# Four steps of a two-stage kernel issued later: a value tile's scaling, its loads, a weight conversion, a group's norms

## The chip, the cores and the metric

One NeuronCore of a Trainium2 chip runs the whole program. The metric is the device time in microseconds (us) of one execution; before the change the median of three runs is 522.26 us (521.84 to 522.62). The engines are called as in the profile: PE is TensorE's matrix multiply and PEld its weight load, DVE is VectorE, ACT is ScalarE, POOL is GpSimd, and SP is the engine that here only issues DMAs. Every engine works through its own instructions in program order; semaphores order them against one another.

## What is computed

A delta rule over 4 batches and 8 heads, with sequences of 768 steps and heads of 48 elements, followed by a feed-forward layer with a maximum of three products:

```python
k_n = k / (norm(k) + 1e-6)
for t in range(S):
    y[t] = q[t] @ state
    state += beta[t] * outer(k_n[t], v[t] - k_n[t] @ state)
x = y.transpose(0, 2, 1, 3).reshape(B * S, H * D)      # 3072 x 384
h = maximum(maximum(x @ w1, x @ w2), x @ w3)           # 3072 x 768
out = h @ w_out                                        # 3072 x 384
```

## The kernel before

**Stages.** The sequence is cut into 12 chunks of 64 steps; two chunks form a group, of which there are six. For a chunk the recurrence becomes products of 64x64 matrices: Gram matrices of keys and queries (`gram`), the inverse of a triangular matrix (`solve`, for a whole group at once, 31 elimination steps of two DVE instructions each, L552 and L556), and then a chain of small matmuls by name: `halves_z`, `halves_u`, `join_z`, `join_u` finish the inverse; `old_k` (p_k, L731) and the subtraction of L743 form the right-hand side in the value tile; `new` (p_u, L759) makes u, copied out by ACT at L764; `step` (p_s, L782) adds to the state at L789; `to_y` (p_y) and `to_x` (p_x) give the layer's input xt. The values have to be multiplied by the norms of their keys first: `scale` (L287) on POOL, called directly or by `prep_values`.

**The layer.** `ffn(m)` is a generator for group m. Each `yield` ends a piece: three matmuls p_h (L914, recorded as six) and what takes them out of PSUM, an ACT copy for the first of a triple (L922), a DVE maximum for the others (L928). For the first group there are 18 pieces 256 wide (pieces 0 to 17, over the blocks f = 0, 1, 2 twice), nine 512 wide (18 to 26), then four output pieces. PSUM has two buffers for p_h and three for the pairs of banks that the chunk's products share.

**Weights.** They come as 64-bit floats and are converted in the kernel, in 24 parts (`pieces`). `fetch` loads one part (L215) into one of five `w_bits` buffers, on the queue given. Each `some(conv, 1)` makes ACT read the next part (L238 to L240) into one of two `mant` buffers, and then issues the previous part's `joined`: a shift on DVE (L250) and an addition on POOL (L254). So the weights of part p are ready only after the call for part p + 1. Piece i of the first nine uses part i.

**The order is written out by hand.** Up to L1065 stands a straight list for group 0. Then the loop of L1126 runs over the pieces of `ffn(0)`, and after each piece issues what tables give for its number: `FIRST` for the second chunk (`queries`; `S1` is one elimination step of `solve(1)`), `EARLY_LINKS` for the group after it, `CONVERTED` for conversions, `FETCHED` for loads on POOL, and single conditions for loads of keys, queries and values. As all engines keep program order, a line's place in the loop is its place in each queue that it uses. A wait of one instruction holds everything issued after it on that engine.

**The places in question.** `load_v` has three value buffers and two DMAs per call (L139), on SP where nothing else is said. `load_v(1)` is issued on POOL at L1038, `scale(1)` follows at L1052. `solve` begins with `norm`: a square root on ACT (L261) of a tile that comes by DMA (`blocks`, L483), then a chain of short DVE instructions. `solve(2)` is begun in piece 20, ahead of "j1 u0", that is of `join_u(3)` (copied out at L716) and `new(2)`.

Of the kernel before, what the change touches and what calls it, by code (L numbers as in the profile page):

```python
# [23 lines left out]
def kernel(  # L24
# [31 lines left out]
    nc = tc.nc  # L56
# [52 lines left out]
    def rows(bb):  # L109
        return slice(C * bb, C * (bb + 1))  # L110
# [6 lines left out]
    def load(src, dst, n, queues):  # L117
        c, g = divmod(n, 2)
        for bb in range(2):
            queues[bb].dma_start(  # L120
                out=dst[rows(bb ^ g), :, 0:D],
                in_=src[2 * bb + g, :, c * C : (c + 1) * C, :].rearrange(
                    "h p d -> p h d"
                ),
            )

    def place(n):
        return n % NK if n < 12 else n % 4

    def load_k(n, queues=one_queue):  # L130
        load(k, kpad[place(n)], n, queues)

    def load_q(n, queues=one_queue):
        load(q, qpad[n % NQ], n, queues)

    def load_v(c, queue=nc.sync):
        vts[c] = work.tile([128, 2, H, D], FP32, name="v_t", bufs=3)
        for bb in range(2):
            queue.dma_start(  # L139
                out=vts[c][rows(bb)].rearrange("p g h d -> p (g h) d"),  # L140
                in_=v[2 * bb : 2 * bb + 2, :, c * C : (c + 1) * C, :].rearrange(
                    "b h p d -> p (b h) d"
                ),
            )
# [66 lines left out]
    def fetch(queue=nc.scalar):  # L211
        if fetched[0] < len(pieces):
            _, src, (a, b) = pieces[fetched[0]]
            st = work.tile([128, 2 * 384], U32, name="w_bits", bufs=5)
            queue.dma_start(  # L215
                out=st.rearrange("p (a b) -> p a b", a=a), in_=src
            )
            staged.append(st)
            fetched[0] += 1

    def weights():

        waiting = None
        for dst, _, (a, b) in pieces:
            bits = staged.popleft().rearrange("p (a b two) -> p a b two", a=a, two=2)
            low, high = bits[:, :, :, 0], bits[:, :, :, 1]
            mant = work.tile([128, 384], U32, name="mant", bufs=2)
            up = work.tile([128, 384], I32, name="up", bufs=2)  # L230
            mant_v = mant.rearrange("p (a b) -> p a b", a=a)
            up_v = up.rearrange("p (a b) -> p a b", a=a)
            halves = [
                up.bitcast(t)[:, i::2].rearrange("p (a b) -> p a b", a=a)
                for i, t in enumerate((I16, FP16))
            ]

            nc.scalar.mul(mant_v.bitcast(FP32), high.bitcast(FP32), 2.0**-112)  # L238
            nc.scalar.mul(halves[0], low, 2.0**-29)
            nc.scalar.mul(halves[1], high.bitcast(FP32), 2.0**-64)  # L240
            if waiting:
                joined(*waiting)
            waiting = dst, mant, mant_v, up_v
            yield
        joined(*waiting)
        yield
# [39 lines left out]
    def scale(c, nrm):  # L286
        nc.gpsimd.tensor_tensor(  # L287
            out=vts[c], in0=vts[c],
            in1=nrm[:, :, :, None].to_broadcast([128, 2, H, D]), op=ALU.mult,
        )  # L290

    def prep_values(c):

        if c in nrms:
            scale(c, nrms.pop(c))


    nrm_0 = const.tile([128, 2, 2, H], FP32, name="nrm_0")
# [8 lines left out]
    def square(name):  # L307
        return work.tile([128, H, C], FP32, name=name, tag="square", bufs=17)
# [180 lines left out]
    def placed(cc, i, copy=nc.vector.tensor_copy, xs_of=slice(0, 2 * H)):  # L489
        bb, half = divmod(i, 2)  # L490
        r = block(bb, half)
        to = ut[cc][r, :, :, BL * half : BL * (half + 1)].rearrange(
            "p g h i -> p (g h) i"
        )
        of = in_rows(xs[0])[r, :, 16 * cc : 16 * (cc + 1)].rearrange("p i x -> p x i")
        copy(to[:, xs_of], of[:, xs_of])
# [130 lines left out]
    def halves_t(c, parts=(0, 1)):  # L627
        if c not in fine:
            fine[c] = [square("t") for g in range(2)]
        src = [ut[c % NU][:, g].rearrange("p h x -> p (h x)") for g in range(2)]  # L630
        dst = [t.rearrange("p h x -> p (h x)") for t in fine[c]]
        if 0 in parts:
            nc.vector.transpose(out=dst[0], in_=src[0])
        for bb in range(2) if 1 in parts else ():
            nc.vector.transpose(out=dst[1][rows(1 - bb)], in_=src[1][rows(bb)])
# [42 lines left out]
    def halves_u(c):  # L678
        t, z = fine.pop(c), zs[c % NU]
        for hs, p_v, negate in negated_of(c, "p_f", BL):  # L680
            for i, h in enumerate(hs):
                for bb, g in TILES:
                    r = rows(bb ^ g)
                    nc.tensor.matmul(p_v[bb][rows(bb), g, i], t[g][r, h], z[r, g, h])
            for f in (0, 1):
                for bb in range(2):
                    r = block(bb, f, HB)
                    negate[bb](
                        ut[c % NU][r, :, span(hs), BL * f + HB : BL * (f + 1)],
                        p_v[bb][r, :, :, HB * f : HB * (f + 1)],  # L690
                        -1.0,
                    )
# [267 lines left out]
    def some(gen, n):  # L960
        for _ in range(n):
            if next(gen, gen) is gen:
                break

    conv = weights()
    solving = solve(0)
# [68 lines left out]
    blocks(1, nc.gpsimd)  # L1035
    for _ in range(2):
        fetch(nc.gpsimd)
    load_v(1, nc.gpsimd)  # L1038
    halves_u(0)
    turn_t1(0)  # L1040
    join_z(0)
# [7 lines left out]
    new(0)  # L1049
    some(conv, 1)  # L1050
    fetch(nc.gpsimd)
    scale(1, nrm_0[:, 1])  # L1052
    placed(1, 3)
    halves_t(1, (0,))
    to_y(0)
    halves_t(1, (1,))
    solving = solve(1)
    some(solving, 1)
    to_x(0)
    fetch(nc.gpsimd)  # L1060
    some(conv, 1)
    fetch(nc.sync)
    some(conv, 1)
    load_q(4)
    load_v(2)  # L1065

# [31 lines left out]
    def links(m, names):  # L1100
        for name in names.split():
            f, i = name[0], int(name[1])
            if f in RECURS and m < GROUPS:
                RECURS[f](2 * m + i)
            elif f in MADE and m + 1 < GROUPS:
                MADE[f](2 * (m + 1) + i)
            elif f in UNIT and m + 1 < GROUPS:
                UNIT[f](4 * (m + 1) + i)
            elif f == "N" and m + 2 < GROUPS:
                load_blocks(4 * (m + 2) + i)  # L1110
# [10 lines left out]

    CONVERTED = {0, *range(2, 6), *range(11, 25)}
    FETCHED = {8: 1, 12: 1, 13: 1, 14: 1, 18: 2, 19: 2, 20: 1, 21: 1}
    for i, _ in enumerate(ffn(0)):  # L1126
        if 0 < i < 7:
            fetch(nc.sync)
        for _ in range(FETCHED.get(i, 0)):
            fetch(nc.gpsimd)  # L1130
        if i == 25:
            some(conv, 1)
        if i == 20:
            solving = solve(2)
            some(solving, 1)
        if i == 21:
            some(solving, 3)
        queries(FIRST.get(i, ""))
        links(1, EARLY_LINKS.get(i, ""))
        if i in CONVERTED:  # L1140
            some(conv, 1)
        if 3 < i < 14:
            some(solving, (3, 2, 2, 2, 3, 3, 3, 3, 2, 2)[i - 4])
        if i in (5, 7):
            prep_values(i // 2)
        if i in (1, 7):
            for n in range(2):
                load_k(8 + 2 * (i > 1) + n, (nc.gpsimd, nc.gpsimd))
        if i == 0:
            load_v(3)  # L1150
        if i in (0, 2):
            load_q(5 + i // 2)
        if i == 11:
            load_q(11, (nc.gpsimd, nc.gpsimd))
        if i in (10, 21):
            load_v(4 + i // 21)
        if i == 18:
            blocks(2)
        if i == 23:
            prep_values(4)  # L1160
        if i > 21:
            some(solving, (3, 2, 3, 2, 2, 5, 5, 5, 4)[i - 22])
        if i in (27, 28, 29):
            load_blocks(i - 15, nc.sync)
        if i in (15, 17, 19, 22, 25, 27):
            less_first((15, 17, 19, 22, 25, 27).index(i))
        if 27 <= i < 30:
            turn_first((2 * (i - 27), 2 * (i - 27) + 1))
# [5 lines left out]
    for m in range(1, GROUPS):  # L1174
        for i, _ in enumerate(ffn(m)):
# [4 lines left out]
            if m + 2 < GROUPS:  # L1180
                if i == 6:
                    blocks(m + 2)
                if i == 8:
                    solving = solve(m + 2)
# [32 lines left out]
```

## Time and profile before

| what | value |
|---|---|
| median of three runs | 522.26 us |
| the profiled execution's own time | 526.19 us |
| its span, first to last instruction | 524.5 us |
| PE busy | 499.9 us, 95% |
| DVE busy | 304.3 us, 58% |
| POOL busy | 191.6 us, 37% |
| ACT busy | 162.8 us, 31% |
| mean granted TensorE clock | 0.954 |

The profiled execution is 3.93 us longer than the median; 1.7 us of its time lie around the span. Sections of the page give busy time by engine, the span in 40 slices (13.1 us each, a digit is tenths), the DMA queues, the chain that ended last, and groups of instructions by line. A timeline row reads: start, duration, engine, line, operation, tile written from tile read, how many; in brackets the idle time of the engine ahead of it and what ended it. A row of waits reads: who waited for whom, total us, times, longest. A row of windows gives the window, its length, the busy time of PE, PEld, DVE, ACT and POOL with their counts, the granted TensorE clock (1.00 is full), the busy share of the DMA engines, and GB/s.

### The profile page before, as it was taken

How to read it: one execution, taken by the hardware profiler on the slowest of the kernel's cores; microseconds unless marked ns; L12 is line 12 of the kernel's file. 1: busy time of each engine (PE TensorE's matmuls, PEld its weight loads, DVE VectorE, ACT ScalarE, POOL GpSimd, SP SyncE). 2: the span in 40 equal slices, each digit the busy share in tenths (PEclk: the TensorE clock that was granted, in tenths of full speed). 3: DMA queues.
4: the chain of work that ended last, by engine and by line, in shares of the span. 5: the costliest groups of instructions: out<-in, count | busy, mean ns of one | idle time of the engine just before them, and what ended most of it. 6: DMA issues, size and time to landing. Idle time of an engine off the chain costs nothing.

```text
span 524.5 us, 18004 instructions
## 1 busy us (share of the span) xinstructions
PE 499.9 (95%) x7836; PEld 309.5 (59%) x7836; DVE 304.3 (58%) x690; ACT 162.8 (31%) x302; POOL 191.6 (37%) x315
## 2 busy tenths in 40 slices
PE   7778699998999999999999999999999999999996
PEld 6666478855656555565555565555665555654453
DVE  5888659875996361599662998554897231111100
ACT  5574664884422142210152200252201411011000
POOL 7444424682374662872295780502230000000000
PEclk9666879997999999999999999999999999999999
DMA  8939939565026762554485453834333202220011
GB/s 110 210 74 188 208 97 165 160 146 167 15 51 163 163 123 52 127 134 114 106 164 119 116 136 92 165 53 91 85 101 94 43 2 63 57 65 0 0 28 32
DMA packets 105565, 53.45 MB, mean 102 GB/s; under 512 B 89712, under 2 KB 99344, under 8 KB 105488
## 3 DMA queue, kind: packets, MB, share of 16 engines
q1 hardware_dynamic: 94016, 31.94, 30.2%
q0 software_dynamic: 9360, 19.98, 16.0%
q8 instruction: 61, 1.00, 0.8%
q10 hardware_dynamic: 2112, 0.39, 0.5%
q14 instruction: 16, 0.13, 0.1%
HBM read 39.17 MB, written 13.11 MB: 100 GB/s over the span
## 4 chain that ended last, share of the span: by engine, by line
PE 86%; DMA 5%; SPq 2%; DVE 2%; ACT 2%; issue 1%; POOL 1%; POOLq 0%; ACTq 0%
PE p_h L914 39%; PE p_o L946 25%; PE p_g L406 4%; DMA v_t<-in_v_dram 3%; PE p_u L759 2%; PE p_m L894 2%; PE p_k L731 2%; PE p_q L731 2%; PE p_y L801 2%; PE p_s L782 2%; SPq L120 2%; PE p_j L714 2%; PE p_z L701 1%; DMA w_bits<-in_moe_w_dram 1%; PE p_t L329 1%
## 5 line engine op out<-in xcount | busy, mean ns | idle before, releaser
L914 PE MATMUL p_h<-xt,w_sb 128*128 128x512 f32 (+1 forms) x522 | 222.4, 571 | 0.7 <-ACT xt L827 0.6
L914 PEld LDWEIGHTS p_h<-xt,w_sb 128*128 128x128 f32 x522 | 97.6, 196 | 87.1 <-issue 79.6
L946 PE MATMUL p_o<-wo_sb,h 128*128 128x384 f32 x288 | 97.8, 489 | 0.0
L928 DVE TENSOR_TENSOR h<-h,p_h 128x512 f32<-128x512 f32 (+1 forms) x48 | 29.7, 618 | 95.9 <-PE p_h L914 93.9
L946 PEld LDWEIGHTS p_o<-wo_sb,h 128*128 128x128 f32 x288 | 53.7, 190 | 35.7 <-issue 0.5
L556 DVE TENSOR_TENSOR y_bl<-y_bl,tmp 128x31 f32<-128x31 f32 (+20 forms) x139 | 52.5, 378 | 4.8
L952 ACT COPY o_sb<-p_o 128x384 f32<-128x384 f32 x24 | 11.5, 479 | 134.2 <-PE p_o L946 128.1
L552 DVE TENSOR_TENSOR tmp<-x_bl,y_bl 128x31 f32<-128x31 f32 (+20 forms) x139 | 50.1, 360 | 4.1
L924 ACT ACTIVATE h<-p_h 128x512 f32<-128x512 f32 x30 | 17.9, 597 | 87.6 <-PE p_h L914 86.1
L946 PE MATMUL p_o<-w_sb,xt 128*128 128x384 f32 x120 | 42.0, 486 | 0.0
L364 POOL DMA_DIRECT2D turned<-in_q_dram x72 | 39.3, 554 | 4.7 <-POOL turned L359 3.1
L254 POOL TENSOR_TENSOR w_sb<-mant,up 128x384 int32<-128x384 int32 x18 | 19.0, 1060 | 39.5 <-DVE mant L250 37.9
L946 PEld LDWEIGHTS p_o<-w_sb,xt 128*128 128x128 f32 x120 | 22.8, 190 | 15.9
L406 PEld LDWEIGHTS p_g<-kqt 48*64 48x64 f32 x1216 | 24.4, 140 | 11.1 <-issue 6.3
L406 PE MATMUL p_g<-kqt 48*64 48x64 f32 (+1 forms) x1216 | 27.8, 240 | 2.2 <-ACT kqt L335 2.2
L120 POOL DMA_DIRECT2D kpad<-in_k_dram x32 | 21.9, 694 | 15.0 <-PE p_s L782 14.1
L789 DVE TENSOR_TENSOR st<-st,p_s 48x768 f32<-48x768 f32 (+1 forms) x18 | 17.1, 950 | 16.5 <-PE p_s L782 16.3
L139 POOL DMA_DIRECT2D v_t<-in_v_dram x14 | 11.6, 832 | 35.0 <-PE p_u L759 35.0
L390 DVE TENSOR_TENSOR pt<-p_g,mask 128x512 f32<-128x512 f32 x20 | 13.8, 691 | 17.4 <-PE p_g L406 17.4
L287 POOL TENSOR_TENSOR v_t<-v_t,nrm 128x768 f32<-128x768 f32 x12 | 17.9, 1498 | 14.8 <-DVE nrm L281 8.9
L359 POOL MEMSET turned<- 128x96 f32 x18 | 3.3, 192 | 48.9 <-DVE kqt L380 48.9
L743 DVE TENSOR_TENSOR v_t<-v_t,p_k 128x768 f32<-128x768 f32 x11 | 10.5, 951 | 15.0 <-PE p_k L731 15.0
(142 smaller groups left out, 616.9 us busy)
## 6 DMA issues: line engine op xcount, KB each, us to landing
out_dram<-o_sb SPq DMA_DIRECT2D x48, 96.0 KB, 2.2
w_bits<-in_moe_w_dram SPq DMA_DIRECT2D x10, 384.0 KB, 7.5
turned<-in_q_dram POOLq DMA_DIRECT2D x72, 48.0 KB, 2.8
w_bits<-in_moe_w_dram POOLq DMA_DIRECT2D x8, 384.0 KB, 5.8
kpad<-in_k_dram POOLq DMA_DIRECT2D x32, 96.0 KB, 4.9
y_x<-y SPq DMA_DIRECT2D x16, 192.0 KB
qall<-y_x SPq DMA_DIRECT2D x32, 96.0 KB, 3.0
v_t<-in_v_dram POOLq DMA_DIRECT2D x14, 192.0 KB, 5.4
```

The source lines that it names most:

```text
L120: queues[bb].dma_start(out=dst[rows(bb ^ g), :, 0:D], in_=src[2 * bb + g, :, c * C : (c + 1) * C, :].rearrange("h p d -> p h d"),)
L254: nc.gpsimd.tensor_tensor(out=dst.bitcast(I32), in0=mant_v.bitcast(I32), in1=up_v, op=ALU.add)
L287: nc.gpsimd.tensor_tensor(out=vts[c], in0=vts[c], in1=nrm[:, :, :, None].to_broadcast([128, 2, H, D]), op=ALU.mult,)
L364: (queue, nc.gpsimd)[i].dma_start(out=t[p0 : p0 + 32, bb, at : at + NP * 2 * D].rearrange("p (j x) -> p j x", j=NP), in_=(k, q)[i][2 * bb ...
L406: nc.tensor.matmul(p_g[rows(bb ^ (g * i)), par, c0 : c0 + C * (1 + whole)], kq[:, 0], kq if whole else kq[:, i],)
L552: nc.vector.tensor_tensor(out=t_v, in0=row.to_broadcast(t_v.shape), in1=column.to_broadcast(t_v.shape), op=ALU.mult,)
L556: nc.vector.tensor_tensor(out=rest, in0=rest, in1=t_v, op=ALU.subtract)
L731: nc.tensor.matmul(p_b[rows(bb), par, c0 : c0 + D], kqt[g][dims(par), j, bb ^ g, i], st[dims(par), bb ^ g, g, j],)
L914: nc.tensor.matmul(p_h, w_sb[i][:, t, f * 128 : (f + 1) * 128], xt[:, t, lo : lo + w], start=(t == 0), stop=(t == KT - 1),)
L924: nc.scalar.activation(out=h, in_=p_h, func=mybir.ActivationFunctionType.Relu)
L928: nc.vector.tensor_tensor(out=h, in0=h, in1=p_h, op=ALU.max)
L946: nc.tensor.matmul(p_o, stays, moves, start=(n == 0), stop=(n == len(terms) - 1))
```

## The change

In the straight list, `load_v(1)` moves from L1038 to the place of `scale(1)` (L1052), and `scale(1)` moves into piece 0 of the loop. The first output's copies (`to_y(0)`) come ahead of both halves of `halves_t(1)`. One `fetch` on POOL, one conversion call and `load_v(2)` leave the list; the fetch comes back on SP in piece 0, the conversion in piece 6, so that every conversion from the fifth to the tenth is issued one place later in the loop. `load_v(2)` comes in piece 3, `load_v(3)` in piece 9 instead of 0, their scalings in pieces 8 and 13 instead of 5 and 7. Keys 8 and 9 load in piece 4 instead of 1, keys 10 and 11 in piece 8 instead of 7. `solve(2)` begins behind `links` of piece 20 instead of ahead of it. No instruction is added or left out.

```diff
@@ straight list
     for _ in range(2):
         fetch(nc.gpsimd)
-    load_v(1, nc.gpsimd)
     halves_u(0)
...
     fetch(nc.gpsimd)
-    scale(1, nrm_0[:, 1])
+    load_v(1, nc.gpsimd)
     placed(1, 3)
-    halves_t(1, (0,))
     to_y(0)
-    halves_t(1, (1,))
+    halves_t(1)
     solving = solve(1)
     some(solving, 1)
     to_x(0)
-    fetch(nc.gpsimd)
     some(conv, 1)
     fetch(nc.sync)
-    some(conv, 1)
     load_q(4)
-    load_v(2)
@@ loop over ffn(0)
-    CONVERTED = {0, *range(2, 6), *range(11, 25)}
+    CONVERTED = {0, *range(2, 7), *range(11, 25)}
...
-        if 0 < i < 7:
+        if i < 7:
             fetch(nc.sync)
+        if i == 0:
+            scale(1, nrm_0[:, 1])
...
-        if i == 20:
-            solving = solve(2)
-            some(solving, 1)
         if i == 21:
             some(solving, 3)
         queries(FIRST.get(i, ""))
         links(1, EARLY_LINKS.get(i, ""))
+        if i == 20:
+            solving = solve(2)
+            some(solving, 1)
         if i in CONVERTED:
             some(conv, 1)
...
-        if i in (5, 7):
-            prep_values(i // 2)
-        if i in (1, 7):
+        if i in (8, 13):
+            prep_values(i // 4)
+        if i in (4, 8):
             for n in range(2):
-                load_k(8 + 2 * (i > 1) + n, (nc.gpsimd, nc.gpsimd))
-        if i == 0:
-            load_v(3)
+                load_k(8 + 2 * (i > 4) + n, (nc.gpsimd, nc.gpsimd))
...
-        if i in (10, 21):
-            load_v(4 + i // 21)
+        if i in (3, 9, 10, 21):
+            load_v((3, 9, 10, 21).index(i) + 2)
```

## The prediction

> **What bounds the kernel now.** I read the 40 slices first, for where TensorE is not full.
>
> ```profile
> PE   7778699998999999999999999999999999999996
> ...
> PEclk9666879997999999999999999999999999999999
> ```
>
> From slice 10 (131 us) on PE is full at full clock, and what is saved ahead of that is kept. The chain that ended last has its non-PE pieces between 30 and 55 us, at 63 to 67 and at 120 to 125. Second, the waits of 40 to 70 us:
>
> ```profile
> ACT mant L238 <- POOL w_sb L254: 6.0, 1, 6.0
> POOL v_t L287 <- DMA v_t<-in_v_dram: 5.8, 1, 5.8
> PE p_j L714 <- issue: 3.6, 1, 3.6
> PE p_f L684 <- ACT z L676: 2.5, 1, 2.5
> ```
>
> Third, the timeline of each pause, in order of time:
>
> ```profile
> 49.13 1.57 POOL L287 TENSOR_TENSOR v_t<-v_t,nrm 128x768 f32<-128x768 f32 x1 [5.84 <-DMA v_t<-in_v_dram]
> ...
> 52.51 0.54 ACT L238 ACTIVATE mant<-w_bits 128x384 f32<-128x384 f32 x1 [5.95 <-POOL w_sb L254]
> ...
> 54.80 1.14 PE L684 MATMUL p_f<-z,t 64*64 64x32 f32 x64 [2.50 <-ACT z L676]
> ...
> 66.42 0.31 PE L714 MATMUL p_j<-z,t 32*32 32x32 f32 x11 [3.56 <-issue]
> ```
> ```profile
> 122.92 0.26 ACT L261 ACTIVATE root_bl<-x_bl 128x32 f32<-128x32 f32 x1 [4.40 <-DMA x_bl<-at_d]
> ...
> 124.42 0.80 ACT L764 COPY u<-p_u 128x768 f32<-128x768 f32 x1
> ...
> 125.27 1.96 PE L782 MATMUL p_s<-u,kmore 64*64 64x48 f32 x64 [2.37 <-ACT u L764]
> ```
>
> Pause A: POOL sits before the second values' scaling until their load lands; the join of weight part 2 queues behind it, ACT's next conversion needs that join's buffer, and the copies of h and z queue behind the conversion, so p_f starts at 54.80. Pause B: 53 matmuls into p_j PE stops for 3.56 us with nothing that it waits for. Pause C: ACT sits before group 2's root; the copy of u, done waiting at 119.5, stands behind it.
>
> Last, windows cut at the clock's steps:
>
> ```profile
> 52.97:56.38 3.41, 1.58 (x108) 1.58 (x111) 1.00 (x2) 3.41 (x9) 2.71 (x4) 1.00 1.28 223
> 56.38:59.80 3.42, 3.42 (x42) 2.44 (x34) 2.42 (x7) 1.16 (x4) 1.45 (x3) 0.51 1.27 158
> 59.80:63.21 3.41, 3.05 (x124) 2.36 (x124) 3.12 (x9) 2.28 (x5) 0.00 (x0) 0.99 1.16 229
> 63.21:66.62 3.41, 0.20 (x11) 0.20 (x10) 3.27 (x9) 0.80 (x2) 0.99 (x1) 1.00 1.18 263
> 66.62:70.03 3.41, 3.41 (x78) 3.02 (x69) 0.89 (x3) 2.52 (x5) 1.00 (x1) 0.51 0.35 88
> ```
>
> A window with PE busy for 1.58 or 0.20 of 3.41 us is followed by half clock, for one window after pause A, for two after B and C; one with 3.05 is not. At half clock a 256-wide piece takes 2.86 us instead of 1.30 to 1.49, p_u 1.89 instead of 1.08. A pause costs its length and then this.
>
> **The straight list.** With to_y ahead of halves_t, DVE's copy of y no longer stands behind a transpose: it starts when p_y ends (41.84) instead of at 42.40, and piece 0 at 44.6 instead of 45.16. The transpose then comes later on DVE, ahead of a norm that starts at 44.4 either way: free. The value load is issued on POOL from 43.3 (end of the fetch at 42.54 + 0.76), two DMAs of 0.84, the last at 44.1. Its landing is the unknown. Bounds: 5.4 us (the page's median for this load on POOL) and 9.4 (this load in the trace). I take 7.9, nearer the crowded row, for the DMA engines' share is over 1.0 here, although SP's 11.02 us of issuing two value tiles are gone. It lands at 52, scaled at 53.6.
>
> POOL joins part 2 as soon as DVE has shifted it, behind the norm (48.8 + 0.35): 49.2 to 50.2, before 52.4. ACT copies h at 47.5, z at 49.9, then converts. p_f follows piece 1 at 51.7, before 54.80; p_k ends at 54.0. The subtraction of L743 needs p_k and the scaled values: 54.3, before 57.21. So 2.9 us are won here, not the 5.84 that POOL sat; each us that the load lands after 52.7 takes one back.
>
> **The conversion one place later** takes most of the rest's slack. Part 4's shift now stands at the end of piece 2's list on DVE. The same list took from 57.21 (L743) to 63.71 (shift): 6.5 us, then 0.35 for the shift, 1.0 on POOL. From 54.3: 62.3 with 0.1 between. PE meanwhile does piece 2, p_z and piece 3 until 57.7, waits for t's transposes (54.3 + 4.55 = 58.85), does p_j and p_q until 60.5, and sits until 62.3: piece 4 starts there, before 68.55. That is a new wait of 1.8 us in place of the old ones. Behind it part 5 is ready at 65.6 by the same count; PE then goes on without a wait through p_u, p_t, piece 5, p_y, piece 6, p_s, piece 7 and p_x, to piece 8 at 74.3, before 81.81: 7.5 us.
>
> Clock: 60.5 to 62.3 leaves a window as busy as 1.6 of 3.4 us, like the row with 1.58. The Trainium skill (TensorE: Matmul & The Clock Gate, Part 1: The HAM clock gate) lets the clock fall only after at least one idle window of about 3.4 us; by that rule a pause of 1.8 costs nothing and the 7.5 stand. The row shows the fall after 1.8 idle us, so I follow the row. Half clock from 63.2, for two windows as in two of the three cases: the end of piece 4, p_u 1.96, p_t 0.74, piece 5 2.9, p_y put piece 6 at 71.0 instead of 68.3: 2.7 lost. Left: 4.8.
>
> **Pause B.** The instruction queue of PE's size (61 packets of 16 KB for 15,672 instructions, 257 each, so one for 128 matmuls and their loads) had a packet at 55.4 and the next at 63.6, inside the pause; the next came at 67.5, just behind it. I read B as a late instruction packet among the loads. The skill says against it that crossing a block is mostly hidden (Runtime: NRT & Kernel Launch, Instruction fetch mechanics); then B has another cause and need not go. In 43 to 66 us the change removes two value tiles (0.79 MB) and four key DMAs (0.39 MB) of about 5 MB moved. I take B as gone; if it stays, 3.56 us from 59.3 lie mostly in the new wait and cost 2.0 beyond it. So the sum takes nothing for B by itself.
>
> **Loads moved.** Keys 8 to 11: four DMAs of 0.69 = 2.76 us of POOL each time, in its idle times of 2.5 to 8.0 us between joins (64 to 93); landing 4.9, needed at pieces 10 to 15. Their waits for the keys' last readers (p_s of pieces 0 and 6) are long over. Values 2 and 3 on SP: behind the fetches, which wait for ACT's conversions; tile 2 has five pieces, tile 3 four (83.55 to 93.82, 10.3 us) against 7.0 to 9.4 to land. Scalings of 1.5 in pieces 8 and 13, in POOL's 8.0 idle us. All at nothing; without that cover, up to 1.5 a scaling and 2.8 for keys, as joins behind them slip. The fetch on SP instead of POOL: 0.6, both idle; nothing.
>
> **Pause C.** The copies of p_j and u no longer stand behind the root: 1.19 + 0.80 from 118.4, u at 120.5, so p_s follows p_g at 122.9 instead of 125.27. The root still runs at 122.9 (its tile's DMA is not moved) and now holds the conversion and h of piece 21, ready at 125.3, needed for piece 23 at 127.4: hidden. What is late next is DVE: its list from 123.21 is unchanged and has no idle time but 0.67 and 0.2 until 167. Its sum to the state ends at 131.3, so p_k starts there instead of at 135.49; L743 ends at 138.2, so p_u starts there instead of at 141.21: 3.0. From piece 25 on 2.8 are left, as the last maximum (151.11, now some 0.7 earlier) comes just at p_o's last term. Bounds: 1.5 if half clock follows the pauses of 1.1 us at p_k and p_u, 4.6 if DVE does not hold.
>
> **Sum.** 4.8 + 2.8 = 7.6 off the profiled execution's 526.19 is 518.6. That execution is 3.9 above the median, and nothing shows where; if it lies in pause B, the timed runs have less to give (below). Off the median: 514.7.
>
> **Rivals.** (1) The clock doesn't fall in the new wait: 7.5 + 2.8 = 10.3, 512.0; for it stands that its windows may fall elsewhere. (2) Pause B is not there, or smaller, in the timed runs, or stays after: with it gone from the kernel before, p_q would end at 64.3 and piece 5 start at 67.4, some 1.5 us behind the new one: 1.5 + 2.8 = 4.3, 518.0; with it staying, 2.8 + 2.8, 516.7. For it: the 3.9 us, and that one packet in seventeen stalls. (3) DVE takes back C too and the load lands at its bound of 9.4 or later: within 1 us of before. (4) Slower: the value load, now issued 4.4 us later behind three weight parts, lands very late. Behind its scaling on POOL queue part 3's join and all later ones, on DVE L743 with all elimination steps and shifts after it. Each us past 52.7 costs one; the 7.6 are used up at a landing of 60.3, and at 62 the time is 524.0. Against it: no load of values in the trace took over 9.4, and this would be 18.
>
> **How the numbers follow.** Likeliest 0.42: 514.7. Rival 1 0.18: 512.0. Rival 2 0.25: 516.7 to 518. Rival 3 0.07, rival 4 0.08. A measurement of this kernel tells about 0.2% (1.0 us) from no change. Faster 0.87, the same 0.05, slower 0.08. The range goes from C's upper bound with rival 1 (510.5) to 520.5, beyond rival 2 with C at its lower bound; it leaves out the end of rival 3 and rival 4.
>
> **What would show it.** Right: POOL's scaling begins at 51 to 54; p_f at about 52 with no wait for z; no wait of ACT for the root ahead of u, p_s at once behind p_g; a PE wait of 1 to 3 us for weights (w_sb, L254) at piece 4. Wrong: the instruction pause of over 2 us still in 50 to 70; DVE's L743 waiting for v_t; pause C giving more than 4.6 or less than 1.5 us; PE pauses behind 131 us that before has not.

## The result, and the profile after

| | before | after |
|---|---|---|
| median, timed side by side | 522.05 us (521.65 to 522.62) | 518.03 us (517.15 to 518.73) |
| ratio, 95% interval | | 0.9921, 0.9903 to 0.9940 |
| the profiled execution's own time, span | 526.19, 524.5 us | 517.84, 515.9 us |

The change makes the kernel 4.1 us (3.1 to 5.1) faster; 7.6 were forecast, and the time lies in the range. Between the two profiled executions the difference is 8.35 us, twice as much. Which of the two is to be explained is the first thing that the runs had to settle. (The ratios below leave out the runs that took over 1.5% longer than the fastest of their kernel, at most two of twelve but four with values only, so they are not the quotients of the medians beside them.)

Two rows of the page after, the 40 slices, answer to the first that were shown of before:

```profile
PE   7877799999999999999999999999999999999996
...
PEclk9657889999999999999999999999999999999999
```

Counted from 0, PE is full from slice 5 (64 us) on and at full clock from slice 6 (77 us); the clock's dip of slice 9 (118 to 131 us) in the profile before is gone. The timeline of the pauses after:

```profile
40.81 1.41 PE L759 MATMUL p_u<-v_t,ut 64*64 64x48 f32 x42 [1.45 <-issue]
...
53.44 1.09 PE L684 MATMUL p_f<-z,t 64*64 64x32 f32 x59 [1.87 <-issue]
...
64.32 2.70 PE L914 MATMUL p_h<-xt,w_sb 128*128 128x256 f32 x6 [1.69 <-POOL w_sb L254]
```
```profile
54.48 1.47 POOL L287 TENSOR_TENSOR v_t<-v_t,nrm 128x768 f32<-128x768 f32 x1 [1.74 <-DMA v_t<-in_v_dram]
```
```profile
115.70 0.80 ACT L764 COPY u<-p_u 128x768 f32<-128x768 f32 x1
116.40 0.26 ACT L261 ACTIVATE root_bl<-x_bl 128x32 f32<-128x32 f32 x1
```

The pause inside p_j is gone. p_f no longer waits for the copy of z, but PE now stops 22 matmuls into chunk 0's p_u and 3 into p_f, again with nothing that it waits for. Piece 4 waits 1.69 us for its weights, as forecast (1.8). POOL's scaling begins at 54.48 instead of the forecast 52, and the root no longer waits at all. Windows of after, cut at the clock's steps:

```profile
61.17:64.58 3.41, 1.72 (x109) 1.56 (x96) 3.27 (x9) 3.35 (x7) 1.00 (x1) 1.00 0.23 60
64.58:67.99 3.41, 3.41 (x46) 2.42 (x49) 2.80 (x9) 1.29 (x3) 1.00 (x1) 0.50 1.12 210
67.99:71.40 3.41, 3.41 (x110) 2.91 (x104) 2.73 (x7) 2.77 (x6) 3.28 (x5) 1.00 0.53 132
```

The window with the new wait has PE busy for 1.72 us and is followed by one at half clock, not two.

A table of where PE stands (start of the first matmul, us) in profiles of before and after carries most of what follows. The last column is the length of the stretch from piece 8 to the first p_o, which holds pause C and nothing of pauses A and B:

| profile | piece 4 | piece 8 | p_s of chunk 2 | first p_o | piece 8 to p_o |
|---|---|---|---|---|---|
| before | 68.55 | 81.8 | 125.27 | 150.7 | 68.9 |
| after | 64.32 | 76.9 | 117.76 | 141.1 | 64.2 |

Read by these two profiles, 4.9 us come from before piece 8 (forecast 4.8) and 4.7 from pause C (forecast 2.8, upper bound 4.6). Of the latter 0.9 is lost again behind the first p_o: from there to the end of the span it is 373.8 us before and 374.8 after.

### The profile page after: what moved, and what is told of

It is laid out like the page before. It is cut to its first block, busy times and chain, and to the rows that moved or that the text cites. A ratio compares the mean times of both kernels' runs of the same rounds, so it can differ in the third digit from the quotient of the medians.

```text
span 515.9 us, 18005 instructions
## 1 busy us (share of the span) xinstructions
PE 494.3 (96%) x7836; PEld 306.2 (59%) x7836; DVE 303.4 (59%) x690; ACT 162.5 (32%) x302; POOL 190.2 (37%) x314
## 4 chain that ended last, share of the span: by engine, by line
PE 81%; DVE 7%; ACT 4%; DMA 2%; SPq 2%; issue 2%; POOL 1%; DVEq 0%; ACTq 0%; POOLq 0%
PE p_h L914 35%; PE p_o L946 26%; PE p_g L406 3%; PE p_u L759 3%; PE p_m L894 2%; PE p_k L731 2%; PE p_y L801 2%; PE p_s L782 2%; SPq L120 2%; PE p_q L731 1%; PE p_j L714 1%; DMA w_bits<-in_moe_w_dram 1%; PE p_z L701 1%; DMA kmore<-in_k_dram 1%; PE p_t L329 1%
## 5 line engine op out<-in xcount | busy, mean ns | idle before, releaser
L914 PE MATMUL p_h<-xt,w_sb 128*128 128x512 f32 (+1 forms) x522 | 218.0, 562 | 2.4 <-POOL w_sb L254 1.7
L914 PEld LDWEIGHTS p_h<-xt,w_sb 128*128 128x128 f32 x522 | 95.6, 192 | 87.1 <-issue 78.1
L552 DVE TENSOR_TENSOR tmp<-x_bl,y_bl 128x31 f32<-128x31 f32 (+20 forms) x139 | 51.5, 370 | 4.1
L556 DVE TENSOR_TENSOR y_bl<-y_bl,tmp 128x31 f32<-128x31 f32 (+20 forms) x139 | 48.5, 349 | 4.8
L759 PEld LDWEIGHTS p_u<-v_t,ut 64*64 64x64 f32 x768 | 13.8, 146 | 10.5 <-issue 8.7
```

What stands on the lines that cost most here:

```text
L552: nc.vector.tensor_tensor(out=t_v, in0=row.to_broadcast(t_v.shape), in1=column.to_broadcast(t_v.shape), op=ALU.mult,)
L556: nc.vector.tensor_tensor(out=rest, in0=rest, in1=t_v, op=ALU.subtract)
L759: nc.tensor.matmul(p_v[rows(bb ^ g), g, i], ut[c % NU][rows(bb), g, h], rhs[rows(bb), g, h],)
L914: nc.tensor.matmul(p_h, w_sb[i][:, t, f * 128 : (f + 1) * 128], xt[:, t, lo : lo + w], start=(t == 0), stop=(t == KT - 1),)
```

## The experiments

**The kernel before once more, and pause C alone.** The first theory was rival 2 with pause C: the long stop in p_j is chance, and the timed gain is mostly C's.

> The kernel before, unchanged, profiled a second time. First theory: the 3.56 us instruction pause inside p_j is chance, and the timed runs mostly go without it: this profile has less than 1.5 us there, piece 5 starts near 67.4 to 69 us instead of 73.87, and the execution's time is near 522. Rival: the pause belongs to this order of loads and is in every run: again 3 us or more inside p_j, piece 5 near 74, time near 526, and the 3.9 us between profile and median are the profiler's.

Unchanged, one profile: 522.92 us.

> The kernel before with solve(2) alone moved behind links of piece 20. First theory: the pause of 2.4 us at p_s and the half clock behind it go, 2.8 to 4.6 us faster than before (ratio 0.991 to 0.995), so most of the whole change's 4.0 us. Rival (the gain lies in the loads, and DVE takes this one back): less than 1.5 us.

```diff
-        if i == 20:
-            solving = solve(2)
-            some(solving, 1)
...
         links(1, EARLY_LINKS.get(i, ""))
+        if i == 20:
+            solving = solve(2)
+            some(solving, 1)
```

> The changed kernel with solve(2) put back ahead of links in piece 20. First theory: what the moves around 40 to 80 us give when the kernel before has no long instruction pause: 0 to 1.5 us faster than before (ratio 0.997 to 1.000); the wait of 2 to 2.5 us at p_s is there again. Rival: 3 us or more faster, as the profiles' 4.9 us at piece 8 say.

The same five lines, undone in the changed kernel.

| kernel | median | before beside it | ratio, 95% interval | profile: piece 8 | piece 8 to p_o |
|---|---|---|---|---|---|
| before again | 522.92 (one) | | | 82.4 | 64.6 |
| solve moved alone | 522.30 | 521.41 | 1.0014, 0.9984 to 1.0044 | 83.0 | 64.4 |
| solve put back | 517.34 | 521.41 | 0.9924, 0.9897 to 0.9952 | 74.7 | 64.1 |

The theory fell on both points. Moving solve(2) alone gains nothing (0.7 us slower, from 0.8 faster to 2.3 slower). With it put back, the rest of the change gives 4.0 us (2.5 to 5.4), the whole gain. And the stop for no visible reason is no single event. The timeline of PE in the second profile of before:

```profile
59.81 1.36 PE L914 MATMUL p_h<-xt,w_sb 128*128 128x256 f32 x3 [2.71 <-issue]
...
67.33 0.42 PE L714 MATMUL p_j<-z,t 32*32 32x32 f32 x11 [2.49 <-issue]
```

and in that of solve moved alone:

```profile
67.86 0.42 PE L714 MATMUL p_j<-z,t 32*32 32x32 f32 x11 [4.50 <-issue]
```

It comes always with 11 matmuls of p_j left, for 3.56, 2.49 and 4.50 us, and in the last two profiles PE stops a second time, 3 matmuls into piece 2 (2.71 and 0.25 us). From p_f's third matmul to piece 2's third are 61 + 64 + 3 = 128, from there to p_j's 53rd 3 + 64 + 6 + 53 = 126: one instruction packet's worth of 128 matmuls within two. That fits a late instruction packet at each place, and the traces hold the packets too. In the first profile of before, the packet that belongs to the stop in p_j landed at 64.83 us, and PE went on at 66.42; in the second, packets landed at 58.24 and 65.70, and PE went on at 59.81 and 67.33. In all fourteen profiles together PE stops 24 times for over 0.2 us at such places between 36 and 72 us, and each stop ends 1.3 to 1.9 us after its packet has landed. So PE stops for its instructions.

What became of pause C stands in ACT's rows. The root in the second profile of before, then in that of solve put back:

```profile
121.69 0.26 ACT L261 ACTIVATE root_bl<-x_bl 128x32 f32<-128x32 f32 x1 [1.93 <-DMA x_bl<-at_d]
121.97 1.18 ACT L716 ACTIVATE ut<-p_j 32x512 f32<-32x512 f32 x2
123.18 0.80 ACT L764 COPY u<-p_u 128x768 f32<-128x768 f32 x1
```
```profile
114.05 0.26 ACT L261 ACTIVATE root_bl<-x_bl 128x32 f32<-128x32 f32 x1 [1.73 <-DMA x_bl<-at_d]
...
115.54 0.80 ACT L764 COPY u<-p_u 128x768 f32<-128x768 f32 x1
```

The root's tile was issued at 114.51 in the first profile of before and used 8.4 us later; here the issues are at 116.00 and 108.12, 5.7 and 5.9 us earlier than the root. With 2.5 to 2.7 us less of DMA the copy of u still comes behind the root, but p_s waits for it not at all here and for 0.57 us with solve put back, and the clock stays full. So the pause that the first profile priced at over 4 us is hidden here behind piece 21 and p_g. One later profile (loads alone, below) has it again, with the tile 7.1 us under way: ACT waits 3.17 us, p_s 1.72, half clock follows, and the last column of the table is 67.2. With solve(2) moved PE has another wait: in all eight such profiles p_u of chunk 3, between 131 and 138 us, waits 0.66 to 1.00 us for L743, and in none of the other six.

**The conversions earlier.** What does the new wait at piece 4 cost?

> The changed kernel with the conversion calls of pieces 2 and 3 issued ahead of those pieces' other work, so that DVE's shifts of weight parts 4 and 5 no longer stand behind transposes, a mask and elimination steps. First theory (piece 4 waits for the late conversion, 1.69 us and half clock behind it): the wait at piece 4 falls below 0.5 us, the clock stays full there, and the time is 1.5 to 4 us below the changed kernel's (ratio to before 0.985 to 0.989). Rival (the slack is eaten by the instruction packets or by DVE): the wait turns up under another name, and the time is within 1 us of the changed kernel's.

```diff
+        if i in (2, 3):
+            some(conv, 1)
         queries(FIRST.get(i, ""))
...
-        if i in CONVERTED:
+        if i in CONVERTED - {2, 3}:
```

515.92 us, ratio 0.9915 (0.9883 to 0.9947). The wait of piece 4 is gone from the profile, piece 8 stands at 76.0. The time had no changed kernel beside it; the run was repeated with one:

> The kernel with the conversion calls of pieces 2 and 3 ahead of those pieces' other work, timed again beside the changed kernel. If the wait for weight part 4 costs what the profiles say: 1 to 3 us below the changed kernel of this call. Rival (DVE and the packets set the stretch): within 0.7 us of it.

> The changed kernel once more, as the measure for the kernel with early conversions: 3 to 5 us faster than before, waits of 1.3 to 1.7 us for weights at piece 4, instruction pauses that differ from the other profiles of it in place or length.

517.65 us (0.9903, 0.9870 to 0.9937) against 518.54 us for the changed kernel (0.9904, 0.9873 to 0.9935). A gain of 1 to 3 us is not shown; the ratios are the same within 0.1 us, each known to about 1.7 us. PE's rows in the repeated kernel say where it may go:

```profile
56.50 0.81 PE L914 MATMUL p_h<-xt,w_sb 128*128 128x256 f32 x3 [0.44 <-issue]
65.98 0.49 PE L759 MATMUL p_u<-v_t,ut 64*64 64x48 f32 x17 [1.55 <-issue]
...
104.92 0.72 PE L701 MATMUL p_z<-ut,at 32*32 32x32 f32 x60 [0.81 <-DMA ut<-y_d]
```

With the weights in time PE reaches chunk 1's p_u sooner, and stops there for its instructions. Still piece 8 stands 1.7 us ahead of where the changed kernel's third profile has it (74.83 against 76.56); of this only 0.3 is left at the first p_o, since p_z then waits for a DMA that in the other profile is in time, and p_u of chunk 3 waits for L743 in both. That is one profile of each, and an argument only; the wait's price stays below what this measurement tells.

**Which part of the rest.** The second theory: the loads, spread out, no longer make the instruction packets late.

> The changed kernel, unchanged, timed and profiled again beside the three below. The theory now (second theory): the gain is that of the stretch from 40 to 80 us, where the loads no longer make PE's instruction packets late in p_j; the root moved in piece 20 gives nothing in most executions. Expected 3 to 5 us faster than before, no instruction pause inside p_j. First theory (half of the gain from the root): also 3 to 5 us here.

> The changed kernel with the loads of values 2 and 3 and of keys 8 to 11, and the scalings 2 and 3, put back to their old places; the straight list, the conversion, value 1 and its scaling stay changed. Second theory (the loads make the instruction packets late): the pause inside p_j or near it is back with 2 to 4.5 us, and at most 1.5 us are left of the gain. Rival (the gain is the scaling of value 1, which no longer holds up POOL, ACT and so p_f): 3 us or more faster than before, no pause in p_j.

```diff
     load_q(4)
+    load_v(2)
...
-        if i in (8, 13):
-            prep_values(i // 4)
-        if i in (4, 8):
+        if i in (5, 7):
+            prep_values(i // 2)
+        if i in (1, 7):
...
+        if i == 0:
+            load_v(3)
...
```

> The kernel before with only the loads of values 2 and 3 and of keys 8 to 11 and the scalings 2 and 3 moved as in the change. Second theory: no pause inside p_j, and 1.5 to 4 us faster than before, while the wait of p_f for the copy of z (0.3 to 2.5 us) stays. Rival (the list's order is what counts): within 1 us of before.

The same lines the other way in the kernel before; value 1's load and scaling and all conversions stay where they were.

> The changed kernel with 0.79 MB of additional copies of values, in packets as those of a value tile, from memory to memory, issued on SP in piece 0; nothing reads them. Second theory: the DMA traffic alone is what delays instruction packets: a pause of 2 to 4.5 us comes back between p_f and p_j, and the time is 2 to 5 us above the changed kernel's. Rival: the packets are late for another reason; no pause over 1.5 us more than in the changed kernel, and less than 1 us lost (the copies hold up only SP's fetches).

```diff
+        if i == 0:
+            for c in range(2):
+                spare = dram.tile([128, 2, H, D], FP32, name="spare")
+                for bb in range(2):
+                    nc.sync.dma_start(
+                        out=spare[rows(bb)].rearrange("p g h d -> p (g h) d"),
+                        in_=v[2 * bb : 2 * bb + 2, :, c * C : (c + 1) * C, :].rearrange(
+                            "b h p d -> p (b h) d"
+                        ),
+                    )
```

Then keys and values were taken apart, each moved alone in the kernel before:

> The kernel before with only the loads of keys 8 to 11 moved to pieces 4 and 8. Third theory (what makes the packets of p_h and p_j late is the traffic between 55 and 66 us, and the two value tiles on SP are what pushes four weight parts into it): the keys alone give 0 to 1.5 us, and pauses of 2 us or more stay between p_f and p_j. Rival (the four key DMAs of 55 to 58 us are what delays the packet of p_j): 2 us or more, no pause over 1 us in p_j.

> The kernel before with only the loads of values 2 and 3 and their scalings moved as in the change; keys 8 to 11 load at their old places. Third theory: most of the gain of loads moved together, 2 to 3.5 us faster than before, instruction pauses of less than 1.5 us in all between p_f and p_j. Rival (keys): less than 1.5 us.

| kernel | median | before beside it | ratio, 95% interval | DMA share, 43 to 66 us | PE's stops without a cause, 36 to 72 us | piece 8 |
|---|---|---|---|---|---|---|
| changed, again | 517.82 | 521.61 | 0.9933, 0.9905 to 0.9962 | 0.53 | p_f 3.24 | 76.8 |
| list only | 520.42 | 521.61 | 0.9988, 0.9964 to 1.0012 | 0.82 | p_u 1.27, p_h 1.76, p_j 0.46 | 78.9 |
| loads only | 517.98 | 521.61 | 0.9942, 0.9911 to 0.9973 | 0.86 | none over 0.3 | 78.1 |
| extra copies | 517.97 | 521.61 | 0.9924, 0.9893 to 0.9955 | 0.63 | p_u 1.27, p_h 1.57 | 78.1 |
| keys only | 520.10 | 522.93 | 0.9941, 0.9917 to 0.9966 | 1.03 | p_h 1.67, p_j 2.72 | 81.7 |
| values only | 522.03 | 522.93 | 0.9948, 0.9914 to 0.9982 | 1.06 | p_j 2.57 | 79.7 |

In the two profiles of before the share is 1.10 and 1.18; in solve put back and in the changed kernel's third profile the stops are p_u 0.89, and p_u 1.70, p_h 1.09, p_j 0.23.

The loads alone give 3.0 us (1.4 to 4.6), the list alone 0.6 (from 1.9 faster to 0.6 slower). So the gain is mostly the loads' (with the two scalings that moved with them), as the second theory said, and not that of the scaling that held up POOL. The rows of PE and POOL with loads only show that pause A is all there and this execution has still no stop in p_j:

```profile
56.10 1.14 PE L684 MATMUL p_f<-z,t 64*64 64x32 f32 x64 [2.66 <-ACT z L676]
```
```profile
50.54 1.47 POOL L287 TENSOR_TENSOR v_t<-v_t,nrm 128x768 f32<-128x768 f32 x1 [6.11 <-DMA v_t<-in_v_dram]
```

But this execution took 521.81 us, as long as before does in the median, with pause C in it as well; it does not show where the other runs gain.

The second half of the theory was that the loads' traffic makes the packets late. With 0.79 MB of copies added in the same packets, the median is that of the changed kernel (517.97 against 517.82; its runs spread wider, 514.38 to 523.17 against 515.74 to 518.93), and the stops are p_u and p_h, none in p_j. That does not settle it: SP issued the copies from 43.9 to 49.6 us, and from 60 to 66 us, where the packet of p_j came in before, the DMA share was 0.05 or less with them, against 1.14 to 1.17 in before. Traffic that ends by 60 us does not bring the loss back; traffic behind 60 us was not added. The third theory, that it is the traffic between 55 and 66 us and mostly the values', missed on the times: keys alone give 3.1 us (1.8 to 4.3), as much as both together. Values alone give 2.7 (0.9 to 4.5) by the ratio, but only 0.9 by the medians of all runs, so their part is not secure. In the one profile of each the stop in p_j is still there:

```profile
66.54 0.42 PE L714 MATMUL p_j<-z,t 32*32 32x32 f32 x11 [2.72 <-issue]
```
```profile
64.49 0.42 PE L714 MATMUL p_j<-z,t 32*32 32x32 f32 x11 [2.57 <-issue]
```

(keys only, then values only). One profile is one draw from runs that differ by 2 to 3 us in standard deviation, so it can't carry that last step.

What the fourteen profiles do show is which of them have the long stop. The packet that holds p_j's last matmuls begins to arrive some time after PE has passed the place in piece 2, 128 matmuls earlier:

| profiles | packet begins after, us | DMA share in the 3.5 us behind that place | stop in p_j, us |
|---|---|---|---|
| before twice, solve moved alone, keys only, values only | 3.8 to 5.5 | 0.85 to 1.15 | 2.5 to 4.5 |
| loads only | 1.6 | 1.13 | none |
| the other eight | 0.2 to 1.6 | 0.02 to 0.69 | 0 to 0.5 |

So the long stop goes with busy DMA engines at this place, as the third theory has it, with one exception. In before SP is held by the two value tiles until 54.3 us and issues four weight parts from 57.5 on, whose traffic fills the stretch; in after its weight parts go out at 43.4, from 47.7 to 54.9 and at 62.1. This is a comparison of profiles and no test.

## Why the prediction was right, and where not

**The size.** 518.03 is 3.3 us above the likeliest case and at rival 2's upper figure (518.0), though for another reason than rival 2's. Its direction and the range held. Of the sum 4.8 + 2.8 the first term is about right in total, 4.0 in the timed runs (solve put back) and 4.9 in the two profiles; the second is the one that was mis-sized. The profiles agree with that: in twelve of the fourteen the execution's own time is 440.1 to 442.1 us more than the start of its piece 8, and the two others (before 444.4, loads only 443.7) are those with a long pause C. So what tells the executions apart lies ahead of piece 8, or is pause C.

**Pause C, 2.8 forecast, nothing measured.** The failed step is "p_s follows p_g at 122.9 instead of 125.27" as something that every execution gives. The row was right for its execution, which had the root's tile 8.4 us under way. With 5.7 to 5.9 the same order costs 0 to 0.6 us and no half clock. Of the six profiles with solve(2) in its old place (before twice, solve put back, loads only, keys only, values only) p_s waits over 1 us in two; in the others it is 0 to 0.6. Where C is hidden, moving solve(2) has nothing to win. "The root still runs at 122.9 (its tile's DMA is not moved)" failed by the same cause: in after the tile was there by 116.4, 1.6 us sooner than the 4.9 us shift accounts for, so DVE started sooner too and took back less than was forecast, 0.91 us before p_u and nothing before p_k.

**The straight list and the conversion, 4.8 forecast, 0.6 alone.** The sum was reached by other parts. The chain POOL, join, conversion, copies, p_f was read rightly, and with it gone p_f does not wait for z any more. But instruction packets took its place: p_f then stood at one (1.87 and 3.24 us in two profiles of the changed kernel), and p_u of chunk 0 stops for 0.9 to 1.7 us in six of the eight profiles with the new list, in none of the six with the old. L743 moved from 57.21 to 56.50 only, not to 54.3. Pause A also varies: p_f waits for z 2.1 to 2.7 us in three of the six profiles with the old list and 0 to 0.34 us in the others, where piece 1 ran at half clock and PE came later; p_f starts at 54.2 to 56.1 us in all six.

That the two profiles give 4.9 us where 4.8 were forecast is partly luck. Full clock began at 44.1 us in after and at 49.6 in before (42.6 to 56.6 in the fourteen), so piece 0 took 1.56 instead of 2.93 us, and no term of the forecast has that.

**Loads at nothing.** The forecast gave the moved loads no term, since it had counted pause B as covered by the new wait ("So the sum takes nothing for B by itself"). That step was wrong: moved alone, they give 3.0 us. Pause B was rightly read as a late instruction packet among the loads. "I take B as gone" holds for p_j, but the stops came back elsewhere: the changed kernel's second profile has 3.24 us in p_f, one of the forecast's own signs of being wrong. That the spread of the loads makes the stops rarer or shorter is supported by the ratios, but not settled (see the end).

**Rival 2** named the right doubt, the 3.9 us between profile and median, with the wrong pause: B was in all three profiles with the old order of loads and list (before twice, solve moved alone), and it was C that most profiles, and it seems most timed runs, lack.

**The new wait for weights** came as forecast, 1.69 us at piece 4 at 64.3 instead of 62.3, and 1.06 to 1.61 in three other profiles of this order. Half clock followed for one window, not for two, and only in two of these four profiles (piece 4 takes 2.70 and 2.93 us); in the other two piece 4 ran at full clock, 1.56 us, as rival 1 had allowed.

**Two slips without weight.** The range's lower end by its own terms is 522.26 - 7.5 - 4.6 = 510.2, not 510.5; and the traffic from 43 to 66 us was 4.35 MB before and 3.07 after, not about 5.

**What stays open.** Why keys alone give what both give together; whether the long stop in p_j is rarer or only shorter when the loads are moved, which would take profiles of many executions of one kernel; and what delays its packet. Weight parts that SP issues late, behind the value tiles, would fit, but an order with these alone moved was not tried.

## What to carry to other kernels

Price a pause from more than one execution before it goes into a sum: in a second profile of the same kernel the three pauses priced here went from 2.50, 3.56 and 2.37 us to 0.34, 2.49 and nothing, and a profile that is 0.8% above the median says that it holds some that the median doesn't. A wait for a DMA with little slack is a chance, not a length. Where short matmuls follow each other at 128 per 3 to 5 us, watch PE's stops "for no cause" by their place: if they return at the same matmuls and each ends just behind a packet of the instruction queue, they are instruction fetches. Moving loads away from them was here worth more (3.0 us) than removing a visible wait (0.6).

## What was unexpected of the hardware

PE's stops lie at fixed matmuls, 128 apart within two, last between 0.2 and 4.5 us, and hop between those places from one execution to the next. The Trainium skill calls crossing such a block mostly hidden (Runtime: NRT & Kernel Launch, Instruction fetch mechanics); in the stretch of small matmuls from 36 to 72 us, 0.9 to 5.2 us of such stops stand in thirteen of the fourteen profiles.

The clock fell after windows with PE busy for 1.54 and 1.72 of 3.41 us in after too, as with 1.58 before; the first of them:

```profile
50.92:54.33 3.41, 1.54 (x66) 1.10 (x68) 2.87 (x9) 1.56 (x3) 0.99 (x1) 1.00 0.59 117
54.33:57.75 3.42, 3.42 (x83) 3.06 (x76) 1.21 (x3) 1.50 (x5) 2.42 (x2) 0.50 0.56 151
```

Between 42 and 132 us of the fourteen profiles, cut at the clock's steps, all thirteen windows at full clock with PE busy for 1.72 us or less were followed by half clock, three of the nine with 1.80 to 2.27, and none with more. So idling for half a window was enough each time, and somewhat less was a matter of chance: solve put back has a wait of 1.61 us at piece 4 in a window with 1.80 us of PE, and keeps full clock.
